# Turning q and x by DMA transposes of 16-bit halves, with GpSimd's copies, and g folded into w1 and w2

## The chip, the core and the metric

The kernel runs on one core of a Trainium2 chip. A core has five engines that run their own instruction streams and wait for each other through semaphores: TensorE (PE in the profile, with its weight loads as PEld), VectorE (DVE), ScalarE (ACT), GpSimd (POOL) and the sync engine (SP), which here only issues transfers. Transfers are carried by sixteen DMA engines. The metric is the device time of one execution in microseconds, as the median of several runs.

## What is computed

A linear attention without softmax, its result normalised over each head and scaled by `g_norm`, is the input `x` of a feed-forward block whose two first products are multiplied with each other.

```python
# q, k, v: (8 batches, 8 heads, 576 tokens, 64); g_norm: (64,)
kv  = np.einsum('bhsd,bhse->bhde', k, v)
out = np.einsum('bhsd,bhde->bhse', q, kv)
rms = np.sqrt(np.mean(out * out, axis=-1, keepdims=True) + 1e-06)
x   = out / rms * g_norm            # then (B,H,S,D) -> (B*S, H*D): 4608 x 512

a = x @ w1                          # w1, w2: 512 x 1024
b = x @ w2
h = (a * b) @ w3                    # w3: 1024 x 1024
result = h @ w_out                  # w_out: 1024 x 512
```

Here q, k, v and g are float32. The four weights come as 64-bit floats and are converted on the chip. The kernel multiplies w3 by w_out first and so has one matrix, `w3o`, for the last two products.

## The kernel before: the parts that matter

Each batch has 576 tokens. 512 of them form one group; the 64 left over of two batches are turned together, and the leftovers of all eight batches form a ninth group. A group goes through `gates` (x by w1 and w2, and the product of the two) and then through a projection by `w3o`. Both products use Winograd's form of Strassen's scheme, so that sums and differences of blocks of x, of w and of w3o are made by VectorE. While one batch is in the gates, the attention of the next is computed in small pieces between the gates' products.

The matmuls want d (the 64 elements of a head) on the partitions, so that q must be turned, and so must x once it is normalised. TensorE turns blocks of 128x128 by multiplying with an identity, and ScalarE copies the result out of PSUM; for x this copy multiplies by g, which then lies along the partitions:

```python
        def q_t(r):
            q_sb = loaded["q", b, r]
            qt_ps = bank(ps_at, "at").rearrange("p (e i t) -> p e i t", e=2, i=2)
            for e in range(2):
                for i in range(2):
                    nc.tensor.transpose(qt_ps[:, e, i, :], q_sb[:, e, i * P:(i + 1) * P], ident)
            qT[r] = work.tile([P, 2, 2, P], FP32, name="qT")
            nc.scalar.copy(qT[r], qt_ps)
# ...
        def turn(r):
            t_ps = bank(ps_at, "at").rearrange("p (j t) -> p j t", j=J)
            m = 2 * (r % 2)
            for j in range(J):
                nc.tensor.transpose(t_ps[:, j, :], st[r // 2][:, j // 2, j % 2, m:m + 2, :], ident)
            dst = xT[b][:, r // 2, :, r % 2, :]
            nc.scalar.activation(
                dst, t_ps.rearrange("p (i j) t -> p i (j t)", i=2), AF.Copy, scale=g_col
            )
        def turn_left():
            t_ps = bank(ps_at, "at").rearrange("p (h r t) -> p h r t", h=2, t=P)
            for r in range(NP):
                nc.tensor.transpose(
                    t_ps[:, r // 2, r % 2, :], st["left"][:, r], ident
                )
            n = b // 2
            dst = x_left[:, :, n // 2, :, (n % 2) * P:(n % 2 + 1) * P]
            nc.scalar.activation(dst, t_ps, AF.Copy, scale=g_col)
```

The products of the attention and the norm between them:

```python
        def norm(o_ps, dsts):
            n, w = len(o_ps), o_ps[0].shape[1]
            inv = work.tile([P, n, w // D], FP32, name="inv")
            for i in range(n):
                sq = work.tile([P, G], FP32, name="sq")[:, 0:w]
                nc.scalar.activation(sq, o_ps[i], AF.Square)
                nc.vector.tensor_reduce(
                    out=inv[:, i], in_=sq.rearrange("p (h d) -> p h d", d=D), axis=AX.X, op=ALU.add
                )
            yield
            nc.scalar.activation(inv, inv, AF.Sqrt, scale=1.0 / D, bias=eps_col)
            yield
            nc.vector.reciprocal(inv, inv)
            for i in range(n):
                m, k = dsts[i].shape[1:3]
                nc.vector.tensor_tensor(
                    out=dsts[i],
                    in0=o_ps[i].rearrange("p (m k d) -> p m k d", k=k, d=D),
                    in1=inv[:, i].rearrange("p (m k) -> p m k", k=k).unsqueeze(3).to_broadcast(
                        [P, m, k, D]
                    ),
                    op=ALU.mult,
                )
# ...
            o_ps = [bank(ps_at, "at") for _ in range(2)]
            for m in range(4):
                r, e = 2 * h + m // 2, m % 2
                for i in range(2):
                    n = 2 * m + i
                    for t in range(2):
                        tokens = slice(t * L, (t + 1) * L)
                        for l in range(2):
                            rows = slice(l * D, (l + 1) * D)
                            nc.tensor.matmul(
                                o_ps[l][tokens, n * D:(n + 1) * D],
                                lhsT=qT[r][rows, e, i, tokens],
                                rhs=kv_b[rows, e, r, :],
                                start=True,
                                stop=True,
                            )
            xn = st[h] = work.tile([P, 2, 2, 4, D], FP32, name="xn", bufs=1)
            return norm(o_ps, [xn[:, :, l].rearrange("p i m d -> p m i d") for l in range(2)])
```

The pieces of a batch, by the place between the gates' products at which they stand (eight places, two for each of the four gates):

```python
    def steps(b):
        a = batch(b)
        a.start()
        more = b + 1 < B
        fs = [[] for _ in range(8)]
        if b == 1:
            fs[0].append((a.begin_kv, 0, 1))
        fs[0].append((a.begin_q, 0, 1))
        fs[1] += [(a.begin_kv, 2, 3), (a.finish, 0)]
        fs[2].append((a.begin_q, 2, 3))
        fs[3] += [(a.turn, 0), (a.turn, 1)]
        if more:
            fs[5].append((batch(b + 1).begin_kv, 0, 1))
        fs[5].append((a.finish, 1))
        fs[7] += [(a.turn, 2), (a.turn, 3)]
        if b % 2:
            fs[2].insert(0, (a.q_t_left,))
            fs[6].append((a.product_left,))
            fs[7].append((a.turn_left,))
            if more:
                fs[7].append((load_q_left, b + 1))
        elif more:
            fs[0].append((load_q_left, b + 1))
        return iter([lambda s=s: [f(*args) for f, *args in s] for s in fs])
```

A gate, its seven products in order (`between` is where a piece stands), and the differences of x that the products need (`combine_x`):

```python
        r1 = product("a11", "b11")
        p1 = keep("p1", r1)                 # keep: ScalarE copies PSUM to SBUF
        r2 = product("s1", "t1")
        p5 = keep("p5", r2)
        product("s2", "t2", r1)
        u2 = keep("u2", r1)
        between()
        product("s4", "b22", r2)
        done("c12", r2, u2)                 # done: VectorE adds, then multiplies the two halves: ab
        product("s3", "t3", r1)
        u3 = keep("u3", r1)
        done("c22", p5, u3)
        r3 = product("a12", "b21")
        done("c11", r3, p1)
        between()
        product("a22", "t4", r1)
        done("c21", r1, None)
# ... combine: t1 = b12 - b11, t2 = b22 - t1, t3 = b22 - b12, t4 = b21 - t2
        return [lambda a=a: nc.vector.tensor_sub(*a) for a in args]
# ... b11 to b22 of x: index i is the half (h) of the heads, j the half (r) within it
        xb[T] = {f"b{i + 1}{j + 1}": xT[T][:, i, j] for i in range(2) for j in range(2)}
```

In the program text `combine_x` of the next group stands in the projection, after its first product. TensorE's instructions keep the order of the text; the order on the other engines is made by a scheduler when the program is built, except in the first stage, where only GpSimd's is.

## Time and profile before

Three runs gave 794.05, 794.41 and 794.48 us. The profiled execution has a span of 792.2 us at a granted TensorE clock of 0.999.

| what | value |
|---|---|
| median of 3 runs | 794.41 us |
| TensorE busy | 784.4 us of 792.2 |
| VectorE, ScalarE busy | 499.0 and 282.2 us |
| GpSimd busy | 24.8 us, 36 instructions |
| turns of q on TensorE (line 297) | 128 instructions |
| turns of x on TensorE (line 381) | 128 instructions |
| turns of leftovers (lines 307, 390) | 16 and 16 instructions |
| chain that ended last: lines 297 and 381 | 1.9% and 1.7% of the span |
| transfers | 117.60 MB, mean 148 GB/s |

In the profile's groups a row names the source line, the engine, the operation, output and inputs, and the shape; then come the time busy and the mean of one in nanoseconds. In a timeline each row has its start and its length in microseconds, and neighbours of one kind are merged.

### The profile page before, as it was taken

The page shows a single profiled execution, that of the slowest core. Times are in us where ns is not written, and L with a number is a line of the kernel's source. Part 1 is how long each engine was busy: PE and PEld are TensorE (multiplying, and loading weights), DVE is VectorE, ACT ScalarE, POOL GpSimd, SP SyncE. Part 2 cuts the span into 40 slices and gives each one's busy share as a digit, 9 for nine tenths or more (in the row PEclk, how much of TensorE's full clock was granted, in tenths as well). Part 3 has the DMA queues.
Part 4 walks back from the last instruction along what each step waited for, and adds up shares of the span by engine and source line. Part 5 has one row for each costly group of instructions (what it writes and reads, how often), then busy time and mean ns, then how long its engine had stood idle before and what let it go on. Part 6 is the DMA issues. An engine that isn't in the chain of part 4 may idle for free.

```text
span 792.2 us, 14634 instructions
## 1 busy us (share of the span) xinstructions
PE 784.4 (99%) x6003; PEld 683.1 (86%) x6003; DVE 499.0 (63%) x1050; ACT 282.2 (36%) x540; POOL 24.8 (3%) x36
## 2 busy tenths in 40 slices
PE   8999999999999999999999999999999999999998
PEld 5455788888899889988998899889988998899897
DVE  7968999425575558555755576457645765485366
ACT  6677643223332433233323332333233322222221
POOL 0010003410000000000000000000000000000000
PEclk9999999999999999999999999999999999999999
DMA  9996653574138412841284119411810180055015
GB/s 321 339 334 178 190 148 127 191 265 157 54 99 305 110 54 84 298 120 54 88 297 129 54 56 314 130 54 67 307 34 2 60 308 12 1 191 189 1 34 186
DMA packets 72582, 117.60 MB, mean 148 GB/s; under 512 B 16452, under 2 KB 60484, under 8 KB 72516
## 3 DMA queue, kind: packets, MB, share of 16 engines
q1 hardware_dynamic: 70064, 101.86, 40.2%
q10 hardware_dynamic: 2452, 14.81, 5.4%
q8 instruction: 47, 0.77, 0.4%
q14 instruction: 19, 0.16, 0.1%
HBM read 100.27 MB, written 16.38 MB: 147 GB/s over the span
## 4 chain that ended last, share of the span: by engine, by line
PE 96%; DMA 3%; ACT 1%; DVE 0%; SPq 0%; issue 0%; DVEq 0%; ACTq 0%
PE mm L499 58%; PE mm L771 22%; PE mm L481 6%; PE at L278 3%; PE at L348 2%; PE at L297 2%; PE at L381 2%; DMA raw<-in_moe_w_dram 2%; DMA raw<-in_moe_w_out_dram 1%; PE at L468 1%; PE mm L823 0%; PE at L366 0%; PE at L390 0%; PE at L307 0%; DVE inv L317 0%; ACT w_sb L149 0%
## 5 line engine op out<-in xcount | busy, mean ns | idle before, releaser
L499 PE MATMUL mm<-xT,w_sb 128*128 128x256 f32 x768 | 176.2, 379 | 0.0
L499 PEld LDWEIGHTS mm<-xT,w_sb 128*128 128x128 f32 x768 | 145.5, 190 | 20.0 <-issue 0.5
L499 PE MATMUL mm<-xc,ws 128*128 128x256 f32 x576 | 130.4, 379 | 0.0
L499 PEld LDWEIGHTS mm<-xc,ws 128*128 128x128 f32 x576 | 109.4, 190 | 15.2 <-ACT p L512 0.3
L637 DVE TENSOR_TENSOR c<-mm,u 128x512 f32<-128x512 f32 x36 | 24.9, 690 | 153.6 <-PE mm L499 153.4
L512 ACT COPY u<-mm 128x512 f32<-128x512 f32 x74 | 43.3, 585 | 146.5 <-PE mm L499 141.9
L512 ACT COPY p<-mm 128x512 f32<-128x512 f32 x74 | 43.3, 585 | 88.0 <-PE mm L499 85.5
L499 PE MATMUL mm<-xc,w_sb 128*128 128x256 f32 x288 | 69.6, 385 | 0.0
L771 PE MATMUL mm<-w3o_sb,raw 128*128 128x128 f32 x500 | 62.2, 275 | 0.0
L481 PE MATMUL mm<-chunks,ab 128*128 128x512 f32 x128 | 60.2, 601 | 1.6 <-ACT chunks L149 1.0
L499 PE MATMUL mm<-xT,ws 128*128 128x256 f32 x256 | 60.9, 381 | 0.4 <-ACT p L512 0.4
L771 PEld LDWEIGHTS mm<-w3o_sb,raw 128*128 128x128 f32 x500 | 59.0, 192 | 0.2
L499 PEld LDWEIGHTS mm<-xc,w_sb 128*128 128x128 f32 x288 | 52.5, 190 | 7.3 <-ACT u L512 0.3
L499 PEld LDWEIGHTS mm<-xT,ws 128*128 128x128 f32 x256 | 47.2, 190 | 6.7 <-ACT p L512 0.8
L638 DVE TENSOR_TENSOR ab<-c 128x256 f32<-128x256 f32 x108 | 46.7, 433 | 3.1
L637 DVE TENSOR_TENSOR c<-p,u 128x512 f32<-128x512 f32 x36 | 24.9, 691 | 35.5 <-ACT u L512 35.5
L771 PE MATMUL mm<-w3o_sb,ab 128*128 128x128 f32 x336 | 43.7, 275 | 0.0
L782 ACT COPY u<-mm 128x512 f32<-128x512 f32 x23 | 13.5, 585 | 83.9 <-DVE raw L795 43.4
L317 DVE TENSOR_REDUCE inv<-sq 128x8 f32<-128x512 f32 (+1 forms) x40 | 23.4, 627 | 31.6 <-ACT sq L316 31.6
L481 PEld LDWEIGHTS mm<-chunks,ab 128*128 128x128 f32 x128 | 21.9, 190 | 22.6 <-issue 15.8
L771 PEld LDWEIGHTS mm<-w3o_sb,ab 128*128 128x128 f32 x336 | 41.0, 192 | 0.3
L633 ACT COPY c<-mm 128x256 f32<-128x256 f32 x36 | 13.4, 372 | 48.4 <-PE mm L499 48.4
(150 smaller groups left out, 1109.9 us busy)
## 6 DMA issues: line engine op xcount, KB each, us to landing
w3o_sb<-w3o_l SPq DMA_DIRECT2D x26, 896.0 KB, 5.3
raw<-in_moe_w_dram SPq DMA_DIRECT2D x31, 512.0 KB, 7.4
raw<-w3o_l SPq DMA_DIRECT2D x13, 896.0 KB, 4.6
w3o_sb<-w3o_l ACTq DMA_DIRECT2D x11, 896.0 KB, 4.6
k_sb<-in_k_dram SPq DMA_DIRECT2D x32, 256.0 KB, 3.9
v_sb<-in_v_dram SPq DMA_DIRECT2D x32, 256.0 KB, 4.6
q_sb<-in_q_dram SPq DMA_DIRECT2D x32, 256.0 KB, 4.1
out_dram<-raw SPq DMA_DIRECT2D x14, 512.0 KB, 5.1
```

Of the source, the lines that this page charges most:

```text
L278: nc.tensor.matmul(kv_ps[e * D:(e + 1) * D, r - rs[0], :], lhsT=k_sb[:, e, cols] if j < J else kl[:, 2 * r + e, :], rhs=v_sb[:, e, cols] i ...
L297: nc.tensor.transpose(qt_ps[:, e, i, :], q_sb[:, e, i * P:(i + 1) * P], ident)
L317: nc.vector.tensor_reduce(out=inv[:, i], in_=sq.rearrange("p (h d) -> p h d", d=D), axis=AX.X, op=ALU.add)
L348: nc.tensor.matmul(o_ps[l][tokens, n * D:(n + 1) * D], lhsT=qT[r][rows, e, i, tokens], rhs=kv_b[rows, e, r, :], start=True, stop=True,)
L381: nc.tensor.transpose(t_ps[:, j, :], st[r // 2][:, j // 2, j % 2, m:m + 2, :], ident)
L481: nc.tensor.matmul(sums_ps[half][m], lhsT=w3T[half, c][:, m, :], rhs=chunks[:, c, 1, :], start=(c == 0), stop=(c == KF - 1),)
L499: nc.tensor.matmul(ps[:, u, :], lhsT=lhsT(a_name, u, c), rhs=rhs(b_name, c),  start=(u == 0 and c == 0 and to is None), stop=(c == chunks ...
L512: nc.scalar.copy(t, ps)
L637: nc.vector.tensor_add(c, one, two)
L638: nc.vector.tensor_mul(dst, c[:, 0, :], c[:, 1, :])
L771: nc.tensor.matmul(to[:, i, :], lhsT=x[:, c, :], rhs=y[:, c, :], start=new and place // 4 not in seen, stop=(c == 1), skip_group_check=True,)
L782: nc.scalar.copy(t[:, 0:4], ps[0])
```

## The change

q is turned from the second batch on, and x with it, without TensorE. A 32-bit element is taken as two 16-bit halves. GpSimd copies the halves into two planes, one DMA transpose issued by the sync engine turns the eight blocks of 128x128 halves, and GpSimd copies the turned planes back into 32-bit words. The copy out of PSUM that multiplied x by g is gone with TensorE's turns, so g is multiplied into w1 and w2 instead, by GpSimd after the conversion (g lies along the partitions of both). The pieces of a batch move to other places, so that each turn has time: q of the first two head pairs of the next batch is turned in the seventh piece. The purpose is to take the turns from TensorE.

Unchanged context is cut where the mark `# ...` stands.

```diff
--- before.py
+++ after.py
# ...
 FP32 = mybir.dt.float32
 U32 = mybir.dt.uint32
+U16 = mybir.dt.uint16
 I64 = mybir.dt.int64
 AF = mybir.ActivationFunctionType
 ALU = mybir.AluOpType
# ...
         float(np.array(bits, np.uint32).view(np.float32)) for bits in (0x38000000, 0x47EFFFFF)
     )
-    def conversion(n, dst, raw, cols=slice(0, 1024)):
+    def conversion(n, dst, raw, cols=slice(0, 1024), scale=None):
         dst, raw = (t if len(t.shape) == 3 else t[:, cols] for t in (dst, raw))
         if raw.dtype == FP32:
             yield
-            nc.vector.tensor_copy(out=dst, in_=raw)
+            if scale is None:
+                nc.vector.tensor_copy(out=dst, in_=raw)
+            else:
+                nc.vector.tensor_scalar(out=dst, in0=raw, scalar1=scale, scalar2=None, op0=ALU.mult)
             return
         words = raw.bitcast(U32).rearrange("p (n w) -> p n w", w=2)
         lo, hi = words[:, :, 0], words[:, :, 1]
# ...
             out=dst_bits, in0=dst_bits, scalar1=3, scalar2=None, op0=ALU.logical_shift_left
         )
         nc.vector.tensor_tensor(out=dst_bits, in0=dst_bits, in1=low_bits, op=ALU.add)
+        if scale is not None:
+            nc.gpsimd.tensor_scalar(out=dst, in0=dst, scalar1=scale, scalar2=None, op0=ALU.mult)
# ...
         what, i = todo[n]
         if what == "w":
-            return [conversion(n, w_sb[:, i].rearrange("p w c f -> p (w c f)"), raws[n])]
+            dst = w_sb[:, i].rearrange("p w c f -> p (w c f)")
+            return [conversion(n, dst, raws[n], scale=g_col)]
         if what == "b":
             return [conversion(n, chunks[:, 2 * i:2 * i + 2, 0, :], raws[n])]
         dst = chunks[:, i].rearrange("p w f -> p (w f)")
# ...
         t = bank(ps_mm, "mm")
         for _ in range(n):
             nc.tensor.matmul(t[:, 0:P], lhsT=ident, rhs=ident, start=True, stop=True)
+    def turn_by_dma(srcs, apart, turned, dsts):
+        def words(t):
+            return t.bitcast(U16).rearrange("p ... (n w) -> p ... n w", w=2)
+        def planes(t, i, n):
+            t = t.bitcast(U16).rearrange("p (w n) -> p w n", w=2)
+            size = 4 * P // n
+            return t[:, :, i * size:(i + 1) * size]
+        for i, src in enumerate(srcs):
+            to = planes(apart, i, len(srcs))
+            if len(src.shape) == 3:
+                src, to = words(src), to.rearrange("p w (a n) -> p w a n", a=src.shape[1])
+                nc.gpsimd.tensor_copy(to, src.rearrange("p a n w -> p w a n"))
+            else:
+                nc.gpsimd.tensor_copy(to, words(src).rearrange("p n w -> p w n"))
+        yield
+        nc.sync.dma_start_transpose(
+            out=turned.bitcast(U16).rearrange("p (a t) -> p a t", t=P), in_=apart.bitcast(U16)
+        )
+        yield
+        for i, dst in enumerate(dsts):
+            src = planes(turned, i, len(dsts))
+            if len(dst.shape) == 3:
+                src = src.rearrange("p w (a n) -> p a n w", a=dst.shape[1])
+            else:
+                src = src.rearrange("p w n -> p n w")
+            nc.gpsimd.tensor_copy(words(dst), src)
     def attention(b):
# ...
             qT[r] = work.tile([P, 2, 2, P], FP32, name="qT")
             nc.scalar.copy(qT[r], qt_ps)
+        def q_by_dma(r):
+            qT[r] = work.tile([P, 2, 2, P], FP32, name="qT")
+            q_sb = loaded["q", b, r].rearrange("p e n -> p (e n)")
+            to = qT[r].rearrange("p e i t -> p (e i t)")
+            all_of(turn_by_dma([q_sb], to, q_sb, [to]))
         st = {}
         def q_t_left():
             st["qT"] = work.tile([P, NP, P], FP32, name="qT_left", bufs=1)
-            qt_ps = bank(ps_at, "at").rearrange("p (r t) -> p r t", r=NP)
-            for r in range(NP):
-                nc.tensor.transpose(qt_ps[:, r, :], q_left[b // 2][:, 2 * r:2 * r + 2, :], ident)
-            nc.scalar.copy(st["qT"], qt_ps)
+            src = q_left[b // 2].rearrange("p h d -> p (h d)")
+            to = st["qT"].rearrange("p r t -> p (r t)")
+            all_of(turn_by_dma([src], to, src, [to]))
         def norm(o_ps, dsts):
# ...
             for j in range(J):
                 nc.tensor.transpose(t_ps[:, j, :], st[r // 2][:, j // 2, j % 2, m:m + 2, :], ident)
             dst = xT[b][:, r // 2, :, r % 2, :]
-            nc.scalar.activation(
-                dst, t_ps.rearrange("p (i j) t -> p i (j t)", i=2), AF.Copy, scale=g_col
-            )
+            nc.scalar.copy(dst, t_ps.rearrange("p (i j) t -> p i (j t)", i=2))
+        def turn_two(h):
+            xn, x = st[h].rearrange("p i l m d -> p (i l) (m d)"), xT[b][:, h]
+            flat = x.rearrange("p i r n -> p (i r n)")
+            turned = st[h].rearrange("p i l m d -> p (i l m d)")
+            half = [slice(r * G, (r + 1) * G) for r in range(2)]
+            turns = [
+                turn_by_dma(
+                    [xn[:, :, r * P:(r + 1) * P]], flat[:, half[r]], turned[:, half[r]], [x[:, :, r]]
+                )
+                for r in range(2)
+            ]
+            for _ in range(2):
+                for t in turns:
+                    next(t)
+            for t in turns:
+                all_of(t)
         def turn_left():
-            t_ps = bank(ps_at, "at").rearrange("p (h r t) -> p h r t", h=2, t=P)
-            for r in range(NP):
-                nc.tensor.transpose(
-                    t_ps[:, r // 2, r % 2, :], st["left"][:, r], ident
-                )
             n = b // 2
-            dst = x_left[:, :, n // 2, :, (n % 2) * P:(n % 2 + 1) * P]
-            nc.scalar.activation(dst, t_ps, AF.Copy, scale=g_col)
+            x = x_left[:, :, n // 2, :, (n % 2) * P:(n % 2 + 1) * P]
+            xn = st["left"].rearrange("p r e d -> p (r e d)")
+            apart = st["qT"].rearrange("p r t -> p (r t)")
+            all_of(turn_by_dma([xn], apart, xn, [x[:, h] for h in range(2)]))
         def load_ahead(names, r):
# ...
         def begin_q(*rs):
             for r in rs:
-                q_t(r)
+                q_by_dma(r)
                 load_ahead("q", r)
         def begin(r):
             begin_kv(r)
-            begin_q(r)
+            q_t(r)
+            load_ahead("q", r)
+        first_done = []
+        def begin_first():
+            if not first_done:
+                first_done.append(begin_q(0, 1))
         def finish(h):
             all_of(product(h))
         return SimpleNamespace(**{f.__name__: f for f in (
-            start, begin_kv, begin_q, begin, product, finish, turn, q_t_left, product_left, turn_left,
+            start, begin_kv, begin_q, begin_first, begin, product, finish, turn, turn_two, q_t_left, product_left,
+            turn_left,
         )})
     batches = {}
# ...
         fs = [[] for _ in range(8)]
         if b == 1:
             fs[0].append((a.begin_kv, 0, 1))
-        fs[0].append((a.begin_q, 0, 1))
         fs[1] += [(a.begin_kv, 2, 3), (a.finish, 0)]
         fs[2].append((a.begin_q, 2, 3))
-        fs[3] += [(a.turn, 0), (a.turn, 1)]
+        fs[3].append((a.turn_two, 0))
         if more:
             fs[5].append((batch(b + 1).begin_kv, 0, 1))
         fs[5].append((a.finish, 1))
-        fs[7] += [(a.turn, 2), (a.turn, 3)]
+        if more:
+            fs[6].append((batch(b + 1).begin_q, 0, 1))
+        fs[6].append((a.turn_two, 1))
         if b % 2:
             fs[2].insert(0, (a.q_t_left,))
-            fs[6].append((a.product_left,))
-            fs[7].append((a.turn_left,))
+            fs[4].append((a.product_left,))
+            fs[6].append((a.turn_left,))
             if more:
                 fs[7].append((load_q_left, b + 1))
         elif more:
# ...
                 }
                 gates(T, p, between, lambda name: all_of(f() for f in following[name]))
                 continue
-            gates(T, p, between if T or p else lambda: None)
+            gates(T, p, between if T or p else lambda: batch(1).begin_first())
             if T == 0:
                 if p + 1 < NF:
                     run(sum_w(p + 1))
```

## The prediction

> **What bounds the kernel now.** I read the page's busy times and the chain that ended last, then the timelines of TensorE and VectorE over one batch, then the small GpSimd groups. The first lines:
>
> ```profile
> PE 784.4 (99%) x6003; PEld 683.1 (86%) x6003; DVE 499.0 (63%) x1050; ACT 282.2 (36%) x540; POOL 24.8 (3%) x36
> PE 96%; DMA 3%; ACT 1%; DVE 0%; SPq 0%; issue 0%; DVEq 0%; ACTq 0%
> ```
>
> TensorE is busy for 99% of the span and makes 96% of the chain, so every instruction taken from it is worth its pitch, as long as nothing else makes it wait. GpSimd is free. Next TensorE's timeline (start, length, instruction), from the last product of a batch's attention to the projection:
>
> ```profile
> 449.71 1.16 PE L348 MATMUL at<-kv_sb,qT 64*64 64x64 f32 x64
> 450.80 1.99 PE L499 MATMUL mm<-xc,w_sb 128*128 128x256 f32 x8
> ...
> 457.90 0.69 PE L366 MATMUL at<-kv_sb,qT_left 64*64 64x64 f32 x32
> ...
> 463.81 1.04 PE L381 MATMUL at<-ident,xn 128*128 128x128 f32 x8
> 464.69 0.60 PE L390 MATMUL at<-ident,xn_left 128*128 128x128 f32 x4
> 465.12 1.89 PE L499 MATMUL mm<-xc,w_sb 128*128 128x256 f32 x8
> 466.85 1.50 PE L771 MATMUL mm<-w3o_sb,ab 128*128 128x128 f32 x12
> ```
>
> Eight transposes hold TensorE from 463.81 to 464.69, 0.88 us, or 0.109 us each; four hold it for 0.43 us. And VectorE's timeline at the same place:
>
> ```profile
> 454.03 1.28 DVE L326 TENSOR_TENSOR xn<-at,inv 128x512 f32<-128x512 f32 x2
> ...
> 462.95 0.69 DVE L637 TENSOR_TENSOR c<-p,u 128x512 f32<-128x512 f32 x1 [0.59 <-ACT u L512]
> 463.67 0.42 DVE L638 TENSOR_TENSOR ab<-c 128x256 f32<-128x256 f32 x1
> 464.13 0.42 DVE L551 TENSOR_TENSOR raw<-ab,ab 128x256 f32<-128x256 f32 x1
> 464.47 0.68 DVE L637 TENSOR_TENSOR c<-mm,p 128x512 f32<-128x512 f32 x1
> 465.07 0.41 DVE L729 TENSOR_TENSOR w3o_sb<-raw 128x256 f32<-128x256 f32 x1
> 465.41 0.42 DVE L638 TENSOR_TENSOR ab<-c 128x256 f32<-128x256 f32 x1
> ```
>
> The `ab` that ends at 465.83 is an operand of the projection's first product, which starts at 466.85: one microsecond to spare. In the windows view VectorE is busy 18.93 of the projection's 21.89 us and 29.63 of the 58.75 us ahead of it. So near the projection VectorE is almost the second bound.
>
> **What the Trainium skill says.** GPSIMD Engine Reference, section 3.1, puts a one-input body at 1.03 cycles an element where its ports are the limit; section 7 puts a read whose step is over 8 bytes at about 2.9 cycles instead of 1.9, half as much again. The trace has no GpSimd copy, but its fills fit one cycle an element:
>
> ```profile
> L242 POOL MEMSET kl_sb<- 64x512 f32 x1 | 0.5, 523 | 0.1
> masks.py:197 POOL MEMSET ident<- 128x128 f32 x1 | 0.2, 204 | 0.3 <-POOLq L1023 0.3
> ```
>
> (523 - 204) / 384 elements is 0.83 ns an element, with 0.10 us fixed. SBUF — State Buffer, "Who interferes with whom", says that a VectorE instruction with two SBUF inputs and a GpSimd instruction that reads SBUF exclude each other; the trace agrees weakly (the GpSimd additions of 128x256 take 726 to 1072 ns in different groups). DMA: Bandwidth & Descriptors, "Latency and other measured facts", gives a DMA transpose 261 GB/s in one case and 350 to 400 at best; no run here shows one yet.
>
> **The change, part by part.**
>
> *Removed from TensorE.* Seven batches (the first keeps its transposes) lose 16 for q and 16 for x, 224; the four pairs of leftovers lose 4 and 4, 32. 256 x 0.109 = **27.9 us**, all on the chain: 794.4 - 27.9 = 766.5.
>
> *Removed from ScalarE.* 28 copies of 0.600, 28 of 0.684, 4 of 0.594 and 4 of 0.688 us, 41 us, all beside TensorE: worth nothing.
>
> *Added.* 64 turns (28 for q, 28 for halves of x, 8 for leftovers), each a GpSimd copy of 1024 16-bit elements into planes, a DMA transpose of 256 KB, and a copy back. Estimates: the first copy (reads 4 bytes apart) 0.10 + 1024 x 0.83 ns = 1.0 us; the copy back reads alternately from two planes 1 KB apart, so half as much again, 0.10 + 1.28 = 1.4 us; the transpose 4.2 us, the landing time of this kernel's 256 KB loads (3.9, 4.6 and 4.1 us for k, v, q), a second one 1 us later. In all 64 x 2.4 = 154 us on an idle engine.
>
> *Where this meets the chain.* I followed the changed program's order on each engine. Take t0, the end of a batch's second product (450.80 above). Only then are the two qT buffers free, and GpSimd's order is: two q copies for the next batch, their two copies back, then the two copies of this batch's xn, and their copies back. From t0:
> - q copies end at 1.0 and 2.0, the first transpose lands at 5.2, the copies back end at 6.6 and 8.0;
> - xn has been ready since 4.5 (455.3), but its copies come now: 9.0 and 10.0; transposes land at 13.2 and 14.2; copies back end at 14.6 and 16.0. With 0.5 us for VectorE's turns at the port, **16.5**.
>
> Who waits: in VectorE's order the subtraction that makes the next batch's `xc` (t2 = b22 - t1) now stands straight after the second addition of the last gate's c22, ahead of the `ab` products for c22 and c11. Before, it stood some twenty instructions later (470.77). That addition starts at 462.95 less 0.63 for the leftover product, which moves to an earlier gate: t0 + 11.5, so the subtraction is reached at 12.2 and held until 16.5. After it come, at the pitches of the trace, xc 0.60, ab 0.34, xT 0.60, raw 0.34, c 0.60, w3o 0.34, ab 0.34: 3.2 us, so the projection's first operand is there at 19.7. TensorE would be ready at 466.85 - 0.63 - 1.31 (its two turns) = t0 + 14.1. It waits 5.6 us. This pattern stands in five batches (turns for batches 2 to 6); batch 1 is turned beside the longer first projection, and the last group's x beside a whole group. 5 x 5.6 = **28 us**.
>
> *The scaling of w by g.* Eight GpSimd passes of about 1 us. The fourth stands in GpSimd's order behind the first q turn, a leftover copy and three additions of the staging. Before, the fourth w was complete at 91.6 us and its sums began at 92.3. After 91.6: third scaling 92.6, two copies 94.6, leftover 95.6, three additions of 0.85 98.1, two copies back 100.9, fourth scaling 101.9, its first sum 102.5. The gate that reads it starts its second product at 98.37: TensorE waits about **4 us**, once.
>
> Sum: 766.5 + 28 + 4 = **798.5 us**, which I round to 798.
>
> **The rivals.**
>
> *Hidden turns.* If copies take 1.0 us both and the transpose 3 us, the chain from t0 reads 4, 6, 8, 10 (first landing), 11, 12, so the subtraction never waits; its two instructions ahead of c11 still cost about 1.3 us a batch. Then 766.5 + 6 + 2 = 775. For it: GpSimd and the DMA are nearly free in the gates (0.34 of DMA time). Against it: two turns in series on one in-order engine.
>
> *Slow GpSimd.* If the 16-bit copies take the 1.9 and 2.9 cycles of the skill's section 7 (1.7 and 2.6 us) and the transpose 5 us, the chain reads 6.7, 11.9, 15.3, 18.6 (first landing at 13.6 + 5), 23.8: wait 12.9 us, five times 64 us, in all 835. For it: elements are scattered in 2-byte steps; both engines want the port. Against it: one-input copies ought to beat the additions' 726 ns for 256 elements.
>
> *The sync queue as the bound.* Transposes are issued by SP in order among loads, and a transpose that waits for GpSimd holds up the loads of the projection's blocks behind it. In the order the projection's loads stand after the second x transpose, which I put at t0 + 10, ahead of the projection's start at 14.1; three blocks are preloaded. I expect no wait here unless the slow rival holds, where it would add a few microseconds a batch.
>
> *VectorE slowed through the port.* About sixteen GpSimd copies a batch fall on a VectorE that is half busy in the gates; what it loses there is mostly absorbed (two PSUM banks of slack), so I give it nothing beyond the 0.5 us above.
>
> **Range and chances.** The wait per batch is (twice the first copy, four copies back, two transposes, each in series) minus a fixed slack, so an error of 1 us in the transpose moves the total by 10 us and 0.3 us in the copy back by 6. The saving of 27.9 us is sure; the cost lies between 8 and 69. Range 772 to 830. Faster by over 2% (below 778.5) needs nearly hidden turns: 0.27. Within 2%: 0.43. Slower (above 810.3): 0.30.
>
> **What would show it.** In the profile after: no q or xn transposes past the first batch, TensorE busy near 757 us; GpSimd at 150 to 200 us; a wait of VectorE's `xc` on GpSimd's copy back of some 4 us in each of five batches, and TensorE idle ahead of the projection with VectorE's `ab` named; one wait of VectorE's `ws` on the scaling near 92 us. If TensorE's idle time is elsewhere (in a product waiting for qT, in a projection waiting for a load), the step on the order is wrong; if it is there but of another size, a duration is.

## The result, and the profile after

The changed kernel takes **842.83 us** (840.04 to 844.59 in four runs) against 794.44 us before: the ratio is 1.0606, with a 95% interval of 1.0575 to 1.0637. It is 48 us slower, and lies above the range of the prediction (772 to 830).

The page of the changed kernel, first the two lines that answer to those shown of before (busy times; the chain that ended last), then three of its GpSimd groups (line, engine, operation, out<-in, count, then busy time and mean of one in ns, then idle time ahead and its releaser):

```profile
PE 779.8 (93%) x5747; PEld 674.4 (80%) x5747; DVE 537.0 (64%) x1050; ACT 245.7 (29%) x476; POOL 201.4 (24%) x176
PE 63%; DMA 10%; DVE 9%; issue 8%; POOL 8%; SPq 1%; ACT 1%; POOLq 0%; DVEq 0%; ACTq 0%
...
L286 POOL COPY qT<-q_sb 128x1024 uint16<-128x1024 uint16 x28 | 30.9, 1127 | 242.1 <-PE at L395 209.0
...
L167 POOL TENSOR_SCALAR w_sb<-w_sb,g_col 128x1024 f32<-128x1024 f32 x8 | 26.6, 3323 | 82.0 <-ACT kv_sb L330 46.8
L298 POOL COPY xT<-xn 128x1024 uint16<-128x1024 uint16 x28 | 34.1, 1246 | 49.8 <-DMA xn<-xT 49.8
```

The 256 transposes are gone (6003 matmul instructions became 5747), yet TensorE's busy time fell by 4.6 us, not 28. Its share of the chain fell from 96% to 63%; GpSimd, the queue's transposes and VectorE have come into the chain. The 16-bit copies last about what was estimated (1.13 and 1.25 us; 1.0 and 1.4 were expected); the scaling of w lasts 3.3 us, not 1.0. And VectorE's busy time rose by 38 us, although its number of instructions is the same.

TensorE's timeline where a projection begins (batch 1; start, length, instruction, and in brackets the idle time ahead and its releaser). Batches are counted from 0, as in the code:

```profile
245.85 1.89 PE L569 MATMUL mm<-xc,w_sb 128*128 128x256 f32 x8
247.58 0.83 PE L841 MATMUL mm<-w3o_sb,ab 128*128 128x128 f32 x6
254.14 1.65 PE L841 MATMUL mm<-w3o_sb,ab 128*128 128x128 f32 x6 [5.72 <-DVE ab L708]
```

Before, the twelve matmuls ran in one piece with VectorE one microsecond ahead. Now TensorE does six and stands for 5.72 us; and the next six take 1.65 us where the first six took 0.83. VectorE's timeline at that place:

```profile
244.95 0.69 DVE L707 TENSOR_TENSOR c<-p,u 128x512 f32<-128x512 f32 x1 [0.76 <-ACT u L582]
250.85 0.69 DVE L611 TENSOR_TENSOR xc<-xT,xc 128x512 f32<-128x512 f32 x1 [5.21 <-POOL xT L298]
251.46 0.42 DVE L708 TENSOR_TENSOR ab<-c 128x256 f32<-128x256 f32 x1
...
253.66 0.42 DVE L708 TENSOR_TENSOR ab<-c 128x256 f32<-128x256 f32 x1
```

The `xc` subtraction for the next batch stands ahead of the two `ab` products and waits 5.21 us for GpSimd. And GpSimd's:

```profile
233.42 2.19 POOL L286 COPY qT<-q_sb 128x1024 uint16<-128x1024 uint16 x2 [10.27 <-issue]
239.39 2.56 POOL L298 COPY qT<-q_sb 128x1024 uint16<-128x1024 uint16 x2 [3.78 <-DMA q_sb<-qT]
241.89 2.02 POOL L284 COPY xT<-xn 128x1024 uint16<-128x1024 uint16 x2
248.57 2.24 POOL L298 COPY xT<-xn 128x1024 uint16<-128x1024 uint16 x2 [4.66 <-DMA xn<-xT]
```

This is the chain of the prediction, almost to the microsecond. With t0 = 233.66 here, the last copy back ends at t0 + 17.15 (predicted 16.5) and the second `ab` at t0 + 20.4 (predicted 19.7).

Where all of the time went is seen from the starts of the stages on TensorE's timeline, each stage counted until the first matmul of the next, the rest until the last matmul; I worked the table out from the timelines of the profiled runs. The stages: the first gates and the first projection (batch 0, with w1 and w2 still being unfolded beside them); the gates of batches 1 to 5; their five projections; and the rest.

| us | first gates | first projection | gates 1-5 | projections 1-5 | rest |
|---|---|---|---|---|---|
| before | 59.4 | 26.3 | 288.7 | 109.4 | 220.6 |
| after | 78.7 | 31.4 | 269.4 | 153.2 | 219.9 |
| difference | **+19.3** | **+5.1** | -19.3 | **+43.8** | -0.7 |

The sum, +48.2, is the whole loss. The saving is there (19.3 in these gates, 4.4 more in the gates of batch 6, offset in the rest). Half of the loss is the five projections, the other half the first two stages.

How full VectorE was in the first gates, the prediction did not look up. The windows view gives it: stretch, length, then busy us and count of TensorE, of its weight loads, of VectorE, ScalarE and GpSimd, then the granted clock of TensorE, DMA share and GB/s. First the kernel before:

```profile
83.90:143.26 59.36, 58.94 (x501) 50.96 (x500) 57.35 (x101) 27.49 (x52) 10.10 (x12) 1.00 0.43 134
```

and the changed kernel:

```profile
83.90:162.61 78.71, 64.29 (x505) 52.96 (x504) 71.29 (x105) 24.23 (x48) 46.34 (x33) 0.89 0.49 128
```

VectorE was busy for 57.35 of 59.36 us, 97%, in a kernel where its mean over the span is 63%. In the changed kernel GpSimd works 36 us more in this stage, and VectorE 14 us more, for nearly the same instructions.

### The profile page after: what moved, and what is told of

It reads as the page before. It is cut to its first block, busy times and chain, and to the rows that moved or that the text cites. A ratio compares the mean times of both kernels' runs of the same rounds, so it can differ in the third digit from the quotient of the medians.

```text
span 840.2 us, 14371 instructions
## 1 busy us (share of the span) xinstructions
PE 779.8 (93%) x5747; PEld 674.4 (80%) x5747; DVE 537.0 (64%) x1050; ACT 245.7 (29%) x476; POOL 201.4 (24%) x176
## 4 chain that ended last, share of the span: by engine, by line
PE 63%; DMA 10%; DVE 9%; issue 8%; POOL 8%; SPq 1%; ACT 1%; POOLq 0%; DVEq 0%; ACTq 0%
PE mm L569 34%; PE mm L841 19%; PE mm L551 5%; DMA q_sb<-qT 3%; DMA xn<-xT 2%; DMA w3o_sb<-w3o_l 2%; POOL xT L284 1%; PE at L319 1%; POOL w_sb L167 1%; DVE ab L708 1%; PE at L395 1%; DMA w3o_l<-stage 1%; POOL qT L298 1%; DVE xc L611 1%; DVE c L707 1%
## 5 line engine op out<-in xcount | busy, mean ns | idle before, releaser
L569 PE MATMUL mm<-xc,ws 128*128 128x256 f32 x576 | 134.1, 386 | 6.1 <-ACT p L582 6.1
L582 ACT COPY u<-mm 128x512 f32<-128x512 f32 x74 | 43.3, 585 | 167.0 <-PE mm L569 137.2
L286 POOL COPY qT<-q_sb 128x1024 uint16<-128x1024 uint16 x28 | 30.9, 1127 | 242.1 <-PE at L395 209.0
L841 PE MATMUL mm<-w3o_sb,ab 128*128 128x128 f32 x336 | 48.4, 290 | 25.3 <-DVE ab L708 24.5
L841 PE MATMUL mm<-w3o_sb,raw 128*128 128x128 f32 x500 | 67.0, 288 | 0.4 <-DMA w3o_sb<-w3o_l 0.4
L841 PEld LDWEIGHTS mm<-w3o_sb,ab 128*128 128x128 f32 x336 | 44.6, 205 | 26.5 <-DVE ab L708 25.3
L841 PEld LDWEIGHTS mm<-w3o_sb,raw 128*128 128x128 f32 x500 | 63.6, 204 | 0.8 <-issue 0.6
L708 DVE TENSOR_TENSOR ab<-c 128x256 f32<-128x256 f32 x108 | 56.2, 520 | 2.9
L167 POOL TENSOR_SCALAR w_sb<-w_sb,g_col 128x1024 f32<-128x1024 f32 x8 | 26.6, 3323 | 82.0 <-ACT kv_sb L330 46.8
L298 POOL COPY xT<-xn 128x1024 uint16<-128x1024 uint16 x28 | 34.1, 1246 | 49.8 <-DMA xn<-xT 49.8
L298 POOL COPY qT<-q_sb 128x1024 uint16<-128x1024 uint16 x28 | 34.0, 1225 | 31.2 <-DMA q_sb<-qT 31.1
```

The lines of the kernel that those rows point to most:

```text
L167: nc.gpsimd.tensor_scalar(out=dst, in0=dst, scalar1=scale, scalar2=None, op0=ALU.mult)
L286: nc.gpsimd.tensor_copy(to, words(src).rearrange("p n w -> p w n"))
L298: nc.gpsimd.tensor_copy(words(dst), src)
L569: nc.tensor.matmul(ps[:, u, :], lhsT=lhsT(a_name, u, c), rhs=rhs(b_name, c),  start=(u == 0 and c == 0 and to is None), stop=(c == chunks ...
L582: nc.scalar.copy(t, ps)
L708: nc.vector.tensor_mul(dst, c[:, 0, :], c[:, 1, :])
```

## The experiments

The theory after the result has three parts. (1) *Order*: in the projections VectorE stands in its queue behind a subtraction that waits for GpSimd, and work that the projection needs stands behind that. (2) *Clock*: after such a gap TensorE runs slower for a while. (3) *First stages*: where VectorE has no slack, GpSimd's work costs time directly, the scaling as well as the copies, by waits and by drawing out VectorE's operations. The rival to all three is that the turns are simply too long, or that GpSimd's sharing of the port slows VectorE everywhere.

Each time below is a median with the ratio to the kernel before in the same set of runs (793.8 to 794.1 us).

### VectorE's order alone

```diff
-        sum_inner(2)
-        for f in ahead:                      # the xc subtractions
-            f()
+        with tc.issue_after(sum_inner(2)):   # queued on VectorE behind these sums
+            for f in ahead:
+                f()
```

> The xc subtractions of the next batch are queued on VectorE behind the inner sums that they stood ahead of; nothing else changes. Theory: the five gaps of 5.7 to 7.4 us before the projections of batches 2 to 6, and the drop of the clock after each, come from VectorE standing still on GpSimd's copy back (16.5 us each) with the additions of ab behind it. Then the copies back still end about 17 us after the product's end, but the wait of the first products on ab is under 1 us in these batches, the five projections take 22 to 23 us instead of 29 to 31, and the time is about 842.8 - 5 x 8.7 = 800 (795 to 806). The loss of 24 us in the stage of w1, w2 and the first projection stays. Rival (the port: GpSimd's and VectorE's shared access slows VectorE's sums themselves): the gaps shrink by 2 us at most, and the time stays above 830.

(The "batches 2 to 6" of this text count from one.) Measured: **805.31 us**, ratio 1.0146 (1.0108 to 1.0183); 37.5 us less than the changed kernel, 43 expected. TensorE's timeline at the same projection:

```profile
248.26 1.50 PE L842 MATMUL mm<-w3o_sb,ab 128*128 128x128 f32 x12
...
250.86 0.71 PE L842 MATMUL mm<-w3o_sb,raw 128*128 128x128 f32 x4 [0.65 <-DVE raw L800]
```

The twelve matmuls are in one piece again. GpSimd's last copy back ends as late as ever (251.82 in this run), so the turns have not become shorter; nothing stands behind them any more. The five projections sum to 116.2 us instead of 153.2. What is left of their loss, 6.8 us, is gaps of up to 0.92 us on inner sums, one of 0.66 us on a load of w3o's blocks, and matmuls that follow VectorE's sums slowly after them (the granted clock is 1.00 all through these projections, so this part is not the clock). VectorE's total busy time is no less (539.4 us), so the port did not make these gaps.

### GpSimd's order alone

```diff
             for _ in range(2):
                 for t in turns:
                     next(t)                # xn: the copies, then the transposes
+            if ahead:
+                with tc.issue_after(last_copy[0]), tc.issue_after(last_dma[0]):
+                    ahead()                # q's copies back
             for t in turns:
                 all_of(t)                  # xn's copies back
...
-            fs[6].append((batch(b + 1).begin_q, 0, 1))
-        fs[6].append((a.turn_two, 1))
+            fs[6].append((batch(b + 1).begin_q_beside, a))
+        else:
+            fs[6].append((a.turn_two, 1))
```

> VectorE's order stays; on GpSimd the copies of xn into 16-bit halves go ahead of q's copies back, and so do xn's transposes on the queue ahead of what follows. Theory: what holds the subtraction is the time at which xn's copy back ends, and this moves from about 17 us to about 12 us after the product's end; the wait of xc becomes 1 to 2 us instead of 4 to 5, and the gap of 5.7 to 7.4 us nearly goes: about 842.8 - 5 x 7 = 808 (800 to 816). Rival (it is the length of the chain of copy, transpose, copy back, not its place behind q's): the end of xn's copy back moves by under 2 us and the time stays above 832.

Measured: **821.34 us**, ratio 1.0336 (1.0312 to 1.036): 21.5 us less, 35 expected. The gaps shrink to 2.65 to 3.67 us (mean 3.0, from 6.4), not to 1. In GpSimd's timeline the copies of xn now wait 2.63 us for VectorE's normalization, which ends at about t0 + 4.5. So time that q's copies back had filled is partly empty now, and going ahead of them brings the end of xn's copy back from t0 + 17.15 to about t0 + 14.1, 3 us sooner instead of 5. Both theories had a share here: the place behind q makes about half of the wait, the chain of copy, transpose and copy back the other half. The remedy on VectorE's side is the better one, since it asks nothing of the chain.

### A filler in the gap

```diff
+        if ahead and T < 6:
+            keep_warm(24)        # 24 matmuls of the identity, ahead of the projection
         r1 = products(0)
```

> 24 matmuls of 128x128 with the identity, whose result nobody reads, stand in TensorE's order ahead of each of the five projections that wait for ab; VectorE and GpSimd are as in the changed kernel, so ab comes no sooner. Theory: the matmuls after a gap of 6 us run at half speed for about 4 us because TensorE stood idle, and this costs 1.6 to 2.4 us a time on top of the gap; with the gap filled the granted clock after it stays near 1 and the time falls by 8 to 12 us (831 to 835). Rival: the slow stretch has another cause (the weights or the operands arriving late, a draw of power that the filler only raises): the time stays at 842 or above.

Measured: 837.66 us (833.29 to 844.57), ratio 1.0556 (1.0502 to 1.061). The interval overlaps that of the changed kernel, so by its time alone this is inconclusive. The profiled run was the slowest of the four. Its traces say more. In the changed kernel the stretch after the gap of batch 1 has a granted clock of 0.62 (same columns as above):

```profile
254.00:258.00 4.00, 3.86 (x22) 3.87 (x23) 4.00 (x13) 0.58 (x1) 0.00 (x0) 0.62 0.01 2
258.00:262.00 4.00, 4.00 (x39) 4.00 (x38) 3.97 (x12) 1.54 (x3) 0.00 (x0) 1.00 0.58 195
```

With the filler, batch 2, TensorE's timeline:

```profile
344.17 0.83 PE L841 MATMUL mm<-w3o_sb,ab 128*128 128x128 f32 x6
346.08 0.94 PE L841 MATMUL mm<-w3o_sb,ab 128*128 128x128 f32 x6 [1.07 <-DVE ab L708]
```

The six matmuls after the rest of the gap, 1.07 us, take 0.94 us, and the granted clock after it is 1.00; in the changed kernel, after 6.39 us, the same six took 1.65. In batch 1 the filler left a gap of 3.14 us, and the clock in the 3.8 us after it is 0.68. Taking the gaps out of the projections' time, what they lose beyond the gaps is 2.3 us each in the changed kernel (153.2 - 109.4 - 32.3 = 11.5 for five), 1.4 with the gaps of 3.0 us in the run before this one, and 1.3 here. So the loss goes with the gaps and shrinks with them, and part (2) holds as far as this. But the clock is not the whole of it: where it stays at 1.00 after a gap, 0.7 us are lost beyond the gap all the same (here after 1.07 us, and in the run before after two of its five gaps), with VectorE busy without a break, so TensorE is then probably fed at VectorE's pace. Nor does the length of the gap alone decide: in the run before, three gaps were of 2.65 us, and the clock in the 4 us after them was 0.57, 1.00 and 1.00; here it was 0.58 after a gap of 2.50 us. In batch 1 the filler's `ab` came 3 us later (after t0) than in the changed kernel, because q's transposes landed later; why, I did not pursue.

### No scaling

```diff
-        if scale is not None:
-            nc.gpsimd.tensor_scalar(out=dst, in0=dst, scalar1=scale, scalar2=None, op0=ALU.mult)
```

This leaves g out of the computation.

> The scaling of w1 and w2 by g on GpSimd is left out (so g is in no product). Theory A: the 24 us lost in the stage of the first w1 and w2 are the eight scalings of 3.3 us, both as waits of the sums behind them and as VectorE's operations drawn out beside them: 15 to 19 us faster, 824 to 828. Theory B: they are the copies of q and x beside VectorE's folds, and the first projection's wait on xn's copies back: 3 to 7 us faster, 836 to 840.

Measured: **828.62 us**, ratio 1.0443 (1.0422 to 1.0464): 14.2 us less. The first gates take 66.7 us instead of 78.7. Leaving the scaling out takes 12.0 us off the loss there. The run as a whole falls just short of theory A's 15 to 19, and the first gates are still 7.3 us longer than in the kernel before, so the scaling is not the whole of it.

### The scaling on ScalarE

```diff
-            nc.gpsimd.tensor_scalar(out=dst, in0=dst, scalar1=scale, scalar2=None, op0=ALU.mult)
+            nc.scalar.activation(dst, dst, AF.Copy, scale=scale)
```

> The scaling of w1 and w2 by g runs on ScalarE (a pass of 128x1024 with a scale per partition) instead of GpSimd; 8 passes of about 1.2 us. Theory: it is GpSimd's slowness and its effect on VectorE, not the existence of the scaling, that costs: within 4 us of the kernel without any scaling. Rival: ScalarE is itself full in this stage (its folds and squares), and its own operations are pushed back: over 6 us slower than the kernel without any scaling.

Measured: **845.60 us**, ratio 1.0656 (1.0631 to 1.0681): 17 us slower than without any scaling. The rival's number is right, its reason only half: ScalarE is not full in this stage (busy for 30.3 of the 73.5 us of the first gates). Its timeline:

```profile
98.15 1.15 ACT L167 ACTIVATE w_sb<-w_sb,g_col 128x1024 f32<-128x1024 f32 x1 [2.90 <-DVE w_sb L165]
99.21 2.03 ACT L556 COPY w3o_sb<-mm 128x512 f32<-128x512 f32 x4
```

and TensorE's:

```profile
99.83 5.77 PE L569 MATMUL mm<-xc,ws 128*128 128x256 f32 x16 [7.17 <-ACT w3o_sb L556]
```

The pass itself takes 1.15 us, a third of GpSimd's. But it waits 2.90 us for VectorE's part of the unfolding, and four copies out of PSUM stand behind it; TensorE stands for 7.17 us, until the first of these copies is done. It is the trap of part (1) on another engine: an instruction with a late operand, put into a queue ahead of instructions that others need. The same happens once ahead of the first gates: a scaling waits 3.35 us for VectorE, and TensorE stands for 4.39 us. These two waits are 11.6 us of the 17; the rest was not followed up.

### Batch 1 turned by TensorE

The attention of batch 1 lies beside the first gates. Here it keeps its transposes on TensorE (40 of the 256), with plain copies, while w1 and w2 are still scaled by GpSimd.

```diff
-                q_by_dma(r)
+                q_t(r) if b < 2 else q_by_dma(r)
...
-        fs[3].append((a.turn_two, 0))
+        fs[3] += [(a.turn, 0), (a.turn, 1)] if b == 1 else [(a.turn_two, 0)]
```

(the same for the left tokens and for the second half of x; the pieces of this batch stand where they stood before.)

> Batch 1, whose attention lies in the stage of the first gates, is turned by TensorE as in the kernel before (q, x and the left tokens); batches 2 to 7 by the transposes of the queue; w1 and w2 are still scaled by GpSimd. Theory: of the 24.4 us lost in the first gates and the first projection 12.0 are the scaling and the other 12.4 are GpSimd's 16-bit copies there, which draw out VectorE's operations in a stage where VectorE is busy 97%, and hold the first projection through xc: 12 us faster than the changed kernel, about 830 (827 to 833), although 32 transposes come back to TensorE. Rival: the copies don't matter there (the delay is the scaling's, in whole): within 3 us of 842.8, or slower by the 4 us of the transposes.

Measured: **828.87 us**, ratio 1.0432 (1.0415 to 1.0449): 14.0 us less, although 40 transposes more. The first gates take 68.2 us instead of 78.7, the first projection 26.3 instead of 31.4, what it took before. Here the scaling is alone in the first stages and costs 8.8 us (68.2 against 59.4 in the first gates); in the run without scaling the copies are alone and cost 12.4 (7.3 in the gates, 5.1 in the projection), although they save 4.4 us of transposes there. Together they cost 24.4, 3.2 more than the two taken singly.

The two cost in different ways. The windows view of the first gates (columns as above), with the copies alone and with the scaling alone:

```profile
84.00:150.67 66.67, 59.45 (x506) 49.77 (x504) 65.96 (x102) 25.05 (x48) 32.24 (x27) 0.95 0.60 148
83.73:151.89 68.16, 61.28 (x501) 52.49 (x500) 57.98 (x100) 27.00 (x52) 30.42 (x17) 0.95 0.35 111
```

With the copies VectorE is busy for 65.96 of 66.67 us, 8.6 us more than before for the same work: its operations are drawn out. With the scaling it is busy for 57.98 us, as before (57.35); there the stage is longer because VectorE's sums `ws` wait for the scaled w, three times, 6.0 us in all.

### Both orders

To VectorE's order in the five projections comes the same in the first.

```diff
-        run(combine_x(1))
+        with tc.issue_after(last_add[0]):    # behind the first projection's last addition
+            run(combine_x(1))
```

The two lines of the changed kernel that this aims at, VectorE's:

```profile
184.01 1.20 DVE L611 TENSOR_TENSOR xc<-xT,xc 128x512 f32<-128x512 f32 x1 [16.51 <-POOL xT L298]
```

and TensorE's, which waits for ScalarE's copy of u, which waits for the addition behind that subtraction:

```profile
188.79 5.40 PE L569 MATMUL mm<-raw,ab 128*128 128x256 f32 x16 [5.29 <-ACT u L582]
```

> To the run with VectorE's order in the projections is added the same for the first one: xc's subtractions are queued behind the first projection's last addition. Theory: the 5.3 us for which TensorE stands in the first projection, and its slow stretch after that, come from the addition of c12 standing behind xc's wait on GpSimd; the first projection takes 26 to 27 us instead of 31.3 and the time falls by about 5 us from 805.3, to 800 (797 to 803). Rival: the addition is late because VectorE has fallen behind in the gates before: within 2 us of 805.

Measured: **797.61 us** (794.35 to 803.35), ratio 1.0049 (1.0033 to 1.0065): 7.7 us less than with the projections' order alone. TensorE's line in this run:

```profile
183.19 3.62 PE L569 MATMUL mm<-raw,ab 128*128 128x256 f32 x16
```

No wait, and 3.62 us instead of 5.40. The first projection takes 24.2 us, less than before (26.3): the 12 transposes that lay in it are gone and the product of the left tokens (32 small matmuls) has moved to the gates. Two changes of VectorE's order, which remove no instruction, give back 45 of the 48 us. The first gates still take 78.2 us; what pays for them is the 23.6 us that the saved transposes bring in the later gates.

### q alone

```diff
-        fs[3].append((a.turn_two, 0))
+        fs[3] += [(a.turn, 0), (a.turn, 1)]          # x on TensorE, g in ScalarE's copy
...
-            return [conversion(n, dst, raws[n], scale=g_col)]
+            return [conversion(n, dst, raws[n])]     # w1 and w2 not scaled
```

> Only q is turned by the queue and GpSimd; x is turned by TensorE with g in ScalarE's copy as in the kernel before, so that w1 and w2 aren't scaled. 128 of the 256 transposes of 0.109 us are gone: 14 us. Theory: q has a whole stage of slack, so nothing waits for it outside the first gates, where VectorE's lost time takes 4 to 6 us and the saving there is not had: about 794 - 14 + 6 = 786 (781 to 791). Rival: any 16-bit copy on GpSimd slows VectorE enough that the saving is eaten in every batch: 794 or slower.

Measured: **785.51 us**, ratio 0.9899 (0.9883 to 0.9915), as expected. The part of the change that has a stage of slack is worth having as it stands: the five projections take 110.0 us (109.4 before), the gates of batches 1 to 5 9.6 us less, and only the first gates are clearly longer (61.2 us, 59.4 before).

### Extra copies, early and late

In the kernel with q alone GpSimd's five first copies of one batch are made four times over (the same data to the same place).

```diff
-            all_of(turn_by_dma([q_sb], to, q_sb, [to]))
+            all_of(turn_by_dma([q_sb], to, q_sb, [to], 4 if b == 1 else 1))
...
-                nc.gpsimd.tensor_copy(to, words(src).rearrange("p n w -> p w n"))
+                for _ in range(times):
+                    nc.gpsimd.tensor_copy(to, words(src).rearrange("p n w -> p w n"))
```

For batch 1, beside the first gates:

> The kernel with q alone by the queue (785.5 us), in which GpSimd's five copies of q for batch 1, the batch turned while the first gates run, are each made four times over: 15 copies of 1.1 us more that write what is there already, and nothing waits for in time. Theory: where VectorE is busy 97% of the stage, GpSimd's copies cost time although nothing waits for them, because VectorE's operations beside them are drawn out: 2 to 6 us slower, 788 to 792. Rival: only waits cost, and there are none here: within 1 us of 785.5.

And with `b == 3`, beside the later gates:

> The same 15 extra copies, for batch 3 instead of batch 1, so that they lie beside the gates of batches 1 and 2, where VectorE is busy under half of the time. Theory: nothing is lost: within 1 us of 785.5. Rival: the copies cost the same wherever they lie: 788 to 792, as in the run beside the first gates.

Measured: early **799.04 us** (797.92 to 799.73; ratio 1.0061, 1.0046 to 1.0076), 13.5 us slower than without them, 0.9 us for each copy; late 787.51 us (ratio 0.9917, 0.9902 to 0.9932), 2.0 us slower. The 15 late copies (three fall into the first projection, six each into the gates of batches 1 and 2) leave these stages as they were: 26.3, 55.3 and 56.6 us, with them and without; what there is in the profiled runs of these 2 us is in the first gates and at the end, where no copy was added, and the intervals of the two ratios overlap. The early ones lengthen the first gates from 61.2 to 76.2 us, over twice what was expected. In no wait of TensorE or VectorE in this stage is GpSimd named; what changes is the length of VectorE's operations, which are busy for 74.4 of the 76.2 us, against 60.3 of 61.2 without the extra copies. VectorE's timeline with the extra copies, and one of GpSimd's beside it:

```profile
84.85 1.50 POOL L287 COPY qT<-q_sb 128x1024 uint16<-128x1024 uint16 x1
85.36 1.52 DVE L617 TENSOR_TENSOR xc<-xT 128x512 f32<-128x512 f32 x1
...
94.47 2.77 DVE L159 TENSOR_SCALAR w_sb<-w_sb 128x1024 f32<-128x1024 f32 x2
```

and the same operations without them:

```profile
83.48 0.68 DVE L616 TENSOR_TENSOR xc<-xT 128x512 f32<-128x512 f32 x1
...
88.17 1.28 DVE L159 TENSOR_SCALAR w_sb<-w_sb 128x1024 f32<-128x1024 f32 x2
```

A subtraction of 0.68 us takes 1.52 us beside a GpSimd copy, 0.84 us more, which is most of a copy's own 1.04 us, and the copy takes 1.50. This fits what the Trainium skill states in SBUF — State Buffer, "Who interferes with whom": a VectorE instruction with two SBUF inputs contends with a GpSimd instruction that reads SBUF, and a pass in the two-port mode does so too, each keeping the other out while it runs. The agreement that the prediction called weak is a strong one here: where VectorE had no slack, each copy cost nearly its full length.

### A version that beats both

From the runs above: batch 1 by TensorE, batches 2 to 7 by the queue and GpSimd; w1 and w2 not scaled, g multiplied into x in place by ScalarE after the copies back, at a place in its queue where they are sure to have come; xc's subtractions behind the inner sums, and behind the first projection's additions.

```diff
+        with tc.issue_after(last_keep[0]):           # ScalarE, behind the third product's copies
+            while to_scale:
+                x = to_scale.pop(0)
+                nc.scalar.activation(x, x, AF.Copy, scale=g_col)
+        with tc.issue_after(sum_inner(4)):           # VectorE, behind the inner sums
+            for f in ahead:
+                f()
```

> All that the runs before point to, together: batches 2 to 7 turned by the queue and GpSimd, batch 1 by TensorE; w1 and w2 not scaled, g multiplied into x by ScalarE in place after the copies back, queued behind the third product's copies in the projection; xc's subtractions queued behind the inner sums of the projection, and behind the first projection's additions. Theory: the first gates and projection take what they did before (85.7 us), each of the gates of batches 1 to 6 is about 4 us shorter than before (24 us), the projections are within 1 us of before's: 794 - 24 + 4 = 774 (769 to 780). Rival: the projections still lose 2 us each to VectorE's operations drawn out beside GpSimd's copies, as in the run with VectorE's order alone: 780 to 788.

Measured: **775.30 us** (774.2 to 776.92), ratio 0.9764 (0.9749 to 0.978). Its busy times and its chain:

```profile
PE 764.1 (99%) x5787; PEld 662.3 (85%) x5787; DVE 520.7 (67%) x1050; ACT 269.4 (35%) x513; POOL 160.5 (21%) x147
PE 93%; DMA 4%; DVE 2%; ACT 1%; issue 0%; SPq 0%; DVEq 0%; ACTq 0%
```

TensorE is at 99% again. The first gates and projection take 59.3 and 26.3 us, as before (59.4 and 26.3); 216 transposes of 0.109 us are 23.5 us, and the kernel gained 18.8 of them. The other 5 us lie in the projections (114.4 us; 109.4 before).

And the same with g in w1 and w2 by GpSimd (xc's subtractions then behind the inner sums as in the first run):

> The fastest version (775.3 us), but with g multiplied into w1 and w2 by GpSimd, as in the change, in place of ScalarE's passes over x. Theory: the scaling alone costs the first gates 12 us here too, as when it was left out of the changed kernel: 787 (785 to 790). Rival: without the other copies beside it, the scaling fits into the stage: 775 to 779.

Measured: **785.14 us**, ratio 0.9896 (0.9872 to 0.992): 9.8 us more, 8.4 of them in the first gates. This agrees with the 8.8 us of the scaling alone, above; the 12 us expected held what it costs beside the copies. VectorE is busy for 57.7 of 67.7 us, so there is room for its work; it is the three waits of `ws` on the scaling, again 6.0 us, that lengthen the stage.

## Why the prediction was wrong

Its sum was 794.4 - 27.9 + 28 + 4 = 798.5; the measured time is 44 us above that. By its own steps:

- **The removed transposes, 27.9 us: right.** The gates of batches 1 to 6 became 23.6 us shorter; with 40 transposes x 0.109 = 4.4 us in the first stages, where the saving was buried, this makes 28.0.
- **GpSimd's copies and the transposes of the queue: right in sum, in part by luck.** Estimated 1.0 and 1.4 us for the copies and 4.2 us to landing; measured 1.13 and 1.25, and 3.3 us. Together with the reading of the order they put the last copy back at t0 + 16.5; it came at 17.15. With the measured sizes the chain as the prediction had it would have ended at about t0 + 15. What it missed: the first transpose of xn was issued only when both copies had been made (t0 + 10.3), and the first copy back began only when the second transpose had landed (t0 + 14.8). The two errors nearly cancelled.
- **"It waits 5.6 us ... 5 x 5.6 = 28 us": right in mechanism, a little small.** Five gaps before `ab`, of 5.72, 6.39, 7.35, 6.38 and 6.03 us, 31.9 us. That VectorE's order makes them is shown by the first run. The place of q's copies ahead of xn's is only half of the wait (the second run).
- **What that step left out: the slow stretch after each gap**, 11.5 us in five projections (perhaps 0.7 us of each is VectorE's pace and not the clock). The sum charged the gap as idle time and nothing after it. The Trainium skill says it in TensorE: Matmul & The Clock Gate, "What's actually happening": after an idle window of about 3.4 us the array runs at half its clock until it has been busy for another. The trace agrees in the factor (six matmuls in 1.65 us instead of 0.83) and in that it is gone within some 4 us (a clock of 0.62, then 1.00). But a drop showed after gaps of 3.14, 2.65 and 2.50 us too, and none after two others of 2.65 us, so here 3.4 us is not a sharp limit.
- **"Eight GpSimd passes of about 1 us": mis-sized threefold.** 3.3 us (2.8 to 4.3). The estimate took GpSimd's fills, 0.83 ns an element, for a pass that reads f32 and multiplies by a number per partition.
- **"TensorE waits about 4 us, once": the step that failed most.** It looked at one wait in the first gates and took the rest of the stage to be as elastic as the later ones. Measured: +19.3 us in the first gates and +5.1 in the first projection, where besides 4.4 us should have been saved. The step expected a wait of `ws` on the scaling, and that is how the scaling costs; but there were three such waits, 6.7 us in sum. What it had no term for is VectorE itself, which was kept busy for 13.9 us more (8.6 with the copies alone) in a stage where it had 2 us to spare.
- **"What it loses there is mostly absorbed ... so I give it nothing beyond the 0.5 us": true in the gates of later batches, false in the first.** The late extra copies cost their stages nothing, the early ones 0.9 us each. This is the second half of the step that failed. The prediction read VectorE's share in the stages of batch 4 (29.63 of 58.75 us) and applied it to a stage whose share was 57.35 of 59.36.
- **The first projection** was taken to be safe, since it is longer. It has the same trap: xc's wait of 16.51 us with an addition behind it.

So of the 44 us some 25 are the first two stages, some 12 the slow stretches, 4 the larger gaps, and the rest in the last batches. Of the rivals, "VectorE slowed through the port" was the one to be taken seriously, for the first gates, one stage of the eighteen; "the sync queue as the bound" showed only as three waits, of 0.40, 0.28 and 0.79 us, on loads of w3o's blocks. TensorE's busy time, put at 757 us, was 779.8, in large part because matmuls at the lower clock count for longer (the mean granted clock was 0.97); in the version at 99% it is 764.1 with 40 transposes more.

## What to carry to other kernels

Moving work to an idle engine is paid for where its results are waited for, not where it runs: when a queue is in order, look up which instruction now stands ahead of the consumer, and queue the late-fed one behind what others need before judging the move (two such changes gave back 45 of 48 us here). An engine's share of the whole span says nothing of a stage: before adding work beside VectorE, read its share in each stage that the work falls into, and where it is near full, charge every GpSimd copy at nearly its length; for a pass in the middle of a chain, count each wait that it makes. And a gap on TensorE cost more than its length here, 2.3 us beyond gaps of 6.4 us and 1.4 beyond gaps of 3.0, so removing a short one is worth more than it seems.

## What the runs showed of the hardware that was not expected

- The GpSimd copy of 1024 16-bit elements that reads alternately from two planes 1 KB apart took 1.15 us when VectorE was quiet (1.25 in the mean for x), hardly more than the one that reads every other element (1.04; 1.13 in the mean for q).
- Beside VectorE's passes in the first gates the same copies took far longer: two copies back of q took 11.52 us in the run with the scaling on ScalarE, and 6.6 us in that without scaling. So GpSimd is held up beside VectorE as well.
- A GpSimd pass over 128x1024 f32 with a number per partition took 3.3 us, ScalarE's 1.15 us.
- A transpose of 128x1024 16-bit elements on the queue landed 3.3 us after its issue, in the range of the kernel's plain loads of the same 256 KB from memory (medians of 2.9 us for q, 4.7 and 4.8 for k and v in the same profile), and occupied the sync engine for 1.23 us or more.
